# A gated mix of a long convolution and a linear attention on one core: wide PSUM pairs, four-term products, and a new order

## The chip, the core and the metric

The kernel runs on one core of one Trainium2 chip. A core has engines with instruction streams of their own: TensorE (PE; its weight loads are shown as PEld), VectorE (DVE), ScalarE (ACT), GpSimd (POOL) and SyncE (SP), which issues most DMAs. They meet through semaphores. The metric is the device time of one execution in microseconds (us). "Before" is the kernel as it stood, "after" the changed one.

## What is computed

The output is `g*a + (1-g)*b` for an input `u` of 2048 rows (time) by 512 columns (channels), all in bf16, where `a` is a state-space long convolution, `b` a linear attention, and `g` a gate with one value per row:

```python
g = _sigmoid((x * gate_w).sum(-1, keepdims=True))            # x is A_u
# a: per channel d, 128 complex states n
K = jnp.einsum("dn,dnl,dn->dl", Cc, jnp.exp(dt * A * l), dt * Bc).real   # 512 x 2048
a = irfft(rfft(pad(u.T, 4096)) * rfft(pad(K, 4096)))[:, :2048].T + u * Dskip
# b: 32 heads of 16, q, k, v = x @ wqkv
pq, pk = q @ w_phi, k @ w_phi                                # per head, 16 x 16
phi = concat(softmax(p), softmax(-p))                        # 32 features, of pq and of pk
num = phi_q @ (phi_k.T @ v);  den = phi_q @ phi_k.sum(rows) + 1e-6
b = (num / den) @ wo
```

## The kernel before

Line numbers are those of the kernel before, as the profile shows them.

**How the work is put in order.** Nothing is issued where it is written. Each piece of work (a group of matmuls, an eviction, a product, a DMA) is a node, made by `Plan.add` (L111) or `Plan.dma` (L132). It names its engine, the nodes it depends on, the buffers that it takes and drops, and for some ACT nodes the activation table set that it needs (`tab`: "T" for sines, "L" for exponentials and logarithms). `Plan.run` (L153) then issues the nodes in the order that the string `ORDER` (L74) gives, two digits in base 64 for each node. That order was made ahead of time by a planner that is not part of the kernel. `SIDES` holds one digit for each movable node: mostly ACT or DVE for a copy out of PSUM (`Plan.copy`, L147: ACT's at L149, DVE's at L151), in some cases DVE or POOL (`Plan.vec`, L144). `RINGS` holds a digit for each node that may take its PSUM tile from one of two rings. `WARM` (all zeros here) could put idle matmuls ahead of some nodes (`heat`).

**PSUM.** The rings are two double banks for the whole kernel ("ps"), two more double banks that change hands: first "p0" (for the preparation), then three single banks "bk" and one bank "acc" (for keys and early queries), and last two double banks "pf".

**Stages.** `prepare` (L199) loads the parameters, builds the Fourier tables and the polar coefficient tables C, D and G (L383 to L438), and transposes the input to xT (L504). Its sines need table set T, its exponentials L. `fold` (L517) multiplies w_phi into the q and k weights (wtp L530, wps L546): WW then holds folded key weights and the value weights, Wqp the folded query weights. `keys_and_spectrum` (L560) takes the input's spectrum in two stages of matmuls (psAu L591, psBu L616) and writes it to DRAM as XUd; the copies of their results are XAu and xst. `attention_keys` (L660) goes through eight pairs of row tiles (128 rows each). For each tile it projects the keys into one bank (pk L709), takes two exponentials of 512 columns for the two signs (Ek L711), sums them (on PE by L730 for pairs with a 1 in `ZPS`, else on DVE), takes the reciprocal by Ln and Exp, projects the values (vp L757), copies them (vb), multiplies them by the reciprocal (vr L766) and adds up kv (kvp L774).

`plan_queries` (L814) takes four query blocks of 512 rows; 0, 1 and 2 are early and take their tiles from "bk", 3 is late and takes double banks. A block projects (pq L843), takes exponentials (Eq L846), computes denominators (zs, L863 to L889) and turns them into the scales apm (aw L899). These go to DRAM as apd (ar) and come back spread over partitions as ax; then DVE multiplies Eq by ax (em L913), and PE makes num (ops L923) and the product with wo (bps L946 to L953). Block 3's gated rows (outL) are stored at L995.

`plan_conv` (L1060) works in 16 units of 32 channels. For a unit the nodes are: sines cs (`plan_tables`, L1008 to L1026), exponentials E (`plan_exp`, L1035 to L1053), two products A1 and A2 (L1101), a sum A3 of their halves (L1112) for some units, two products R (L1119, L1123), the matmuls kps of the convolution kernel (`kgen_chunk`, L175, L183), its copy KD, the first Fourier stage psA (L190) and its copy XA. Twelve units go by fours through `transform` (L1193), 128 columns of the output at a time; the last block is cut into units (12, 13), 14 and 15. `transform` does the second Fourier stage psB (L196), its copy XK, the products t with the spectrum XUX (L1233, L1236), the first inverse stage psz (L1265), its copy Zr, a transposition over DRAM (Zd written, ZT read, L1287), for the last piece of work a near path without DRAM, the second inverse stage psy, and the mix with the gate (ou, L1362 to L1371), whose rows are stored at L1382.

Whether A3 is issued hangs on the string `FOURS`, one digit a unit: with a 0 the two halves of A are added on DVE and PE takes two product terms, with a 1 PE takes four:

```python
terms = [(k, k) for k in range(2)] if not four else [(0, 0), (2, 0), (1, 1), (3, 1)]
an.append(P.add("DVE", "A3", (lambda: None) if four else a3, an[-1:]))
```

**Table sets.** ACT holds one table set at a time. The loads (L65, by `act.begin`) are nodes of their own, `tabT` and `tabL`, at the places where `prepare` and `phase` (L1076) put them: one T for the first sines, then L, then T for the coefficients, and so on; in the convolution the sines of four units are one phase, with a load on both sides of it.

Of the kernel before, what the change touches and what calls it, by code (L numbers as in the profile page):

```python
# [70 lines left out]
class Plan:  # L71

    DIGITS = "0123456789abcdefghijklmnopqrstuvwxyzABCDEFGHIJKLMNOPQRSTUVWXYZ-_"
    ORDER = ("040B0H0K0d0y0C0D0L0s0I070J0M0P0g000S110j0N08010z0T0m0Q0e2R0a0p0q0r0_0W2T100U0O0V14120Y2U2x0A2S050k130Z2y2V2X2Z0R190v0t0u"  # L74
             "0b0c0w2_0l0E0X2W1516172L1a061b2Y022-30311y33340n030f0-"
             "0h1e1f0i1w2J18321c0F0o2B2K2M1n1z1H1g1A1o2D2C1d1p1I091x1E1J351Q1R2F1B0x1C2E0G2H1q36372G2I2P382N2Q391F3b2O3c4C1S3a4J4L4K4M"
             "3d3e4Q4R3f4U1Y3g4N1r4O1h4V3h1L4Y4-"
             "4P3i4Z4_3j4W4S53542z57504T3k4X1Z515b5d58521s1D593l5c3n5i5e55565j3m5a1G3o5q5f5g5s5r5t3p3r3q1T5m5n5u3s5v5h5o5k5w5x5B1P4D4E"
             "3w2v5l5p4F5y5F5C3y1U5H3x5G5I5J5z5A1V5D5E3t3z5U3D5K5V5M5N3A3R3E2w3F5W5L1O5_3G5O5Q5X5Y5Z3B3C1W605R5S1N3K3M1K3S1M5-"
             "5P3L634G642A615T653N673T6869626a666m6n6o3U6p3V3W3X3Y6b6c6q6d6r6s1t3Z3H3-1X3_3O1i1j41401_4221431-"  # L80
             "1k1l204445466e272923222b282d4748243P491m2a4a2c2e4b4g2f4c2g4d252h2o4e4h4i4n1u4j3u3v2j4p2i2l2k2m2q2p6i262s4q4o1v4k2n4u2r2t"
             "6f4v4w6j4r3I2u4x4y4z6g4l8l3J4A8p8m6t6u6k6v8q3Q4f4s6x6h8k8o6l8n8r8s6y6z6w6A6C4m4t4B8C6G8t6I6K8w8x8y8u6B6H6J4H8D8v6L6M6N7d"
             "8z8A8E4I8B7e7f8I7g8F6F9e8Q8G8H9b6O6P8R7h7j7i6Q6R8J9f7M7N8S6S6T6U6Vaeaf7O8W8X8K7k9g8L8T8U8Z8-"
             "938M8N7l6D8_7m8V7n6W6X6Y8O8P8Y7P94an7o7pao7q6_70717r90917Qa47S9295ag7R6Z7s6-"
             "72aha8a9966Ea7akaca5ai73aa75979998ajap7677a69aalatamab74ad7TaBaC7t797u7v7U78au7y7z7V7w7x9caq9naras7AavaH7W9d9h9o9paw7X9v"
             "aY9waK7Y7ZaDaL9q9raZ7a9x9y9zaIc57B7-aM9kc69D9EaQaEbX9L7Cb_aF7D9M7_9Ac07EaRaG9iaxaz80ay9B818285bYaA7Ga-"
             "7IaJ86879j9Fc19s7Jb-"
             "9l9m9Na_7bc7aNaOaPc3cbb2b37HbZc283aS9C7FaT849G9H9I9t89aUaWaV8baX7cccc8c99O9u9P9Q9R888cb87Kb9b0c4caceb19J8abacfcgbg8dck9K"
             "8ecl8f8gbbbh8hbcbibob4cP9Sbpbqcd9T8ichci7L8jcBcCcjcsdYcYctcucycDczdZd-cQcR9Ucmd_cHcvcw9W9Xcnbj9VbwbkblbxcocIbre0eLcp9Ze1"
             "e2b5b6eMbse3eUeVcxb7bye4cqbtbu9Ybdbe9-"  # L90
             "9_cAcrcSbme5cZdOdScEbfcFcGcTcUe6a0a1bve7dTdRdWeNa2e8cJcKe9bzbAedeecLeRcNcOa3eSeaebeOcMc_ePbBd0ecd1d7cVd8d9cWeCdfcXeWdPdU"
             "d2daefege-e_eQd3dbdQdgeTdVd4dndodXdhdcg1g2dieDeEdjeXbKfAbCbnbDbEbFeYfBeZf0f1bGc-dpbLddg7dqbHd5f2drbMf3f4f5bNfGbIbJbOezdk"
             "eAfDdsfEeBeIf6f7feffdldtbPdebQdBfCfHehdueifFejdmf8fgeJd6ekdvfIfJdyf9fafhfbg4fifKg5g6dwfjdzfkfcdxdCdEfLdAdFfMg3g8dGg9dHfN"
             "fleFelfdfmfpdDdLgagbgcgddIeGemeKfqeHfOfPfQfRgeenepfneofreqeresgfggghgifSfTfUfofsbRgjbSgkdJftetglfVfYfZgmgngobUbVgqfufWdM"
             "dNbWgpf-fvfxfygreufwevewexbTeydKfzfXf_g0gvgwgsgtgugx")
    SIDES = ("011111010010101011001110110010011001010100001011100000000000011000011001111101000100000100000000000000000000000010000000"
             "00100001000000000000000101010000000000000100001101001")
    RINGS = ("001010111111010010100000000000000000000000100000000000000000001101100000000101101011100100100001101010111100111001010100"
             "01111")
    WARM = ("000000000000000000000000000000000000000000000000000000000000000000000000000000000000000000000000000000000000000000000000"  # L100
            "000000000000000000000")
    FOURS = ("0111100101011000")
    ZPS = ("01000111")

    HOT = ("pk", "vp", "pq", "zp", "ops", "bps4", "psA", "psBu", "psB128", "psB64", "psB32", "psz", "pszn", "psyn32", "psy128", "psy64", "psy32", "kps")
# [5 lines left out]
    def add(self, eng, name, fn, deps=(), take=(), drop=(), rw=("", ""), tab=None, sets=None, opens=None, cost=0.0):  # L111
        n = Bag()
        n.eng, n.name, n.fn, n.take, n.drop, n.cost = eng, name, fn, list(take), list(drop), cost
        n.tab, n.sets, n.opens, n.ring = tab, sets, opens, None
# [38 lines left out]
    def run(self):  # L153
# [3 lines left out]
        sides, rings, warm = iter(self.SIDES), iter(self.RINGS), iter(self.WARM)  # L157
        for n in self.nodes:
            n.at = n.eng if isinstance(n.eng, str) else n.eng[int(next(sides, 0))]
            for r in n.take:  # L160
                if not isinstance(r, str):
                    n.ring = r[int(next(rings, 0))]
                elif r in self.psums:
                    n.ring = r
            n.warm = int(next(warm, 0)) if n.name in self.HOT and n.ring in ("ps", "bk", "pf") else 0
        done = set()
# [393 lines left out]
def keys_and_spectrum(P, nc, g, psum):  # L560
# [3 lines left out]
    def bank(name):  # L564
        return g.heat(g.psA.tile([128, 512], F32, name=name, tag="bk"), 2)
# [1062 lines left out]
```

## Time and profile before

| | |
|---|---|
| median of 3 runs | 265.99 us (265.86 to 266.54) |
| the profiled execution | 265.5 us |
| its span in the profile | 263.7 us |
| mean granted TensorE clock | 0.916 |
| DMA | 35.93 MB in 67547 packets, 136 GB/s in the mean |

The profiled execution's span is what the profile's times count from and to; the device time is a little longer. In a row of a timeline stand the start, the duration, the engine, the line, the operation, the tiles written and read with their shapes, the count of instructions that the row sums up, and in brackets an idle time ahead of it with the instruction that ended it. A duration runs from an instruction's start to its end; the next of the same engine may start before that end. A row of a group has the busy time, the mean ns of one, and the idle time ahead of the group.

### The profile page before, as it was taken

To read this page: it belongs to the slowest core of one execution; us is meant where nothing else is said; L and a number is where in the kernel's file an instruction comes from. 1 tells how busy PE (TensorE), PEld (TensorE's weight loads), DVE (VectorE), ACT (ScalarE), POOL (GpSimd) and SP (SyncE) were. 2 spreads that over 40 slices of the span, in tenths; PEclk is the share of its full clock that TensorE was granted. 3 is DMA by queue.
4 is the path that set the end of the run, shared out by engine and by line. 5 is a ranking of instruction groups with operands and counts; after the bars stand their busy time and mean duration, and the time that the engine had idled before them with its cause. 6 is when DMAs were issued, how large, how long until landed. Compare 5 with 4: busy or idle time off the path is not lost.

```text
span 263.7 us, 10050 instructions
## 1 busy us (share of the span) xinstructions
PE 198.5 (75%) x4491; PEld 133.8 (51%) x4512; DVE 233.9 (89%) x315; ACT 221.3 (84%) x305; POOL 8.3 (3%) x21
## 2 busy tenths in 40 slices
PE   0755999999845688988565867889996678979770
PEld 0654656646634423446354245665674456764550
DVE  6799989888799989999999999999999999986630
ACT  6989999998899989998999899999998996744200
POOL 4700000000000000000000000000000000000000
PEclk9999999999995659997999579999999999998975
DMA  6899000454500885203343366239753599989576
GB/s 196 144 204 233 6 4 2 121 146 138 151 10 2 239 239 165 83 13 87 88 162 82 122 209 210 73 116 199 150 193 120 189 239 242 179 206 141 133 112 102
DMA packets 67547, 35.93 MB, mean 136 GB/s; under 512 B 46000, under 2 KB 62000, under 8 KB 67504
## 3 DMA queue, kind: packets, MB, share of 16 engines
q1 hardware_dynamic: 65648, 34.76, 55.0%
q10 hardware_dynamic: 1856, 0.52, 1.1%
q8 instruction: 35, 0.57, 1.0%
q14 instruction: 8, 0.07, 0.1%
HBM read 22.17 MB, written 13.11 MB: 134 GB/s over the span
## 4 chain that ended last, share of the span: by engine, by line
PE 32%; DVE 26%; ACT 13%; DMA 12%; issue 7%; SPq 7%; DVEq 0%; ACTq 0%
PE pk L709 5%; DMA ax<-apd 5%; PE vp L757 5%; DVE A L1101 3%; SPq L1494 3%; DMA ZT<-Zd 3%; DMA apd<-apm 3%; ACT cs L68 3%; DVE R L1123 2%; DVE R L1119 2%; PE psz L1265 2%; PE psA L591 2%; PE bps L946 2%; PE psB L616 2%; PE kvp L774 2%
## 5 line engine op out<-in xcount | busy, mean ns | idle before, releaser
L1101 DVE TENSOR_TENSOR A<-Ctab,Dtab 128x2048 bf16<-128x2048 bf16 x32 | 37.9, 1220 | 0.0
L68 ACT ACTIVATE cs<-args 128x1024 bf16<-128x1024 f32 x32 | 30.8, 1042 | 1.5 <-PE args L1023 1.5
L1265 PE MATMUL psz<-t,TI 128*128 128x512 bf16 x51 | 16.5, 414 | 6.2 <-DVE t L1233 4.6
L1123 DVE TENSOR_TENSOR R<-E,cs 128x2048 bf16<-128x2048 bf16 x16 | 19.5, 1219 | 0.1
L1119 DVE TENSOR_TENSOR R<-E,cs 128x2048 bf16<-128x2048 bf16 x16 | 19.5, 1219 | 0.0
L68 ACT ACTIVATE Ek<-pk 128x512 bf16<-128x512 f32 x32 | 16.7, 600 | 1.9 <-PE pk L709 1.6
L183 PE MATMUL kps<-R,A 128*32 128x64 bf16 x1536 | 17.2, 203 | 1.5 <-DVE A L1112 0.4
L183 PEld LDWEIGHTS <-A 128*32 128x32 bf16 x1536 | 15.3, 117 | 5.6 <-issue 2.0
L149 ACT CAST Zr<-psz 128x1024 bf16<-128x1024 f32 x15 | 15.5, 1032 | 3.2 <-PE psz L1265 1.5
L149 ACT CAST XA<-psA 128x1024 bf16<-128x1024 f32 (+1 forms) x15 | 14.7, 1017 | 3.4 <-PE psA L190 3.4
L757 PE MATMUL vp<-WW,xT 128*128 128x512 bf16 x59 | 16.9, 419 | 0.5 <-issue 0.3
L616 PE MATMUL psB<-XAu,TB 64*128 64x128 bf16 x256 | 11.8, 250 | 6.6 <-ACT xst L149 3.5
L1233 DVE TENSOR_TENSOR t<-XUX,XK 128x2048 bf16<-128x2048 bf16 x14 | 16.7, 1219 | 0.0
L68 ACT ACTIVATE E<-args 128x1024 bf16<-128x1024 f32 x16 | 16.4, 1036 | 0.3 <-PE args L1045 0.2
L68 ACT ACTIVATE Eq<-pq 128x512 bf16<-128x512 f32 (+1 forms) x28 | 16.5, 694 | 0.1
L149 ACT CAST XK<-psB 128x1024 bf16<-128x1024 f32 (+1 forms) x14 | 13.7, 993 | 2.8 <-PE psB L196 1.5
L843 PE MATMUL pq<-xT,Wqp 128*128 128x512 bf16 x64 | 15.4, 379 | 0.8 <-ACT xT L149 0.6
L709 PE MATMUL pk<-WW,xT 128*128 128x512 bf16 x58 | 15.0, 380 | 0.4 <-issue 0.2
L190 PE MATMUL psA<-W,KD 128*64 128x128 bf16 x256 | 10.7, 233 | 5.5 <-ACT KD L149 2.7
L616 PEld LDWEIGHTS <-TB 64*128 64x128 bf16 x256 | 9.7, 111 | 9.9 <-issue 9.8
L196 PE MATMUL psB<-XA,TB 128*128 128x128 bf16 (+2 forms) x192 | 10.6, 206 | 3.6 <-DVE XA L151 1.6
L190 PEld LDWEIGHTS <-KD 128*64 128x64 bf16 x256 | 8.5, 117 | 9.1 <-issue 5.2
(210 smaller groups left out, 502.0 us busy)
## 6 DMA issues: line engine op xcount, KB each, us to landing
XUX<-XUd SPq DMA_DIRECT2D x32, 256.0 KB
XUd<-xst SPq DMA_DIRECT2D x8, 512.0 KB
ax<-apd SPq DMA_DIRECT2D x16, 256.0 KB
Zd<-Zr SPq DMA_DIRECT2D x15, 256.0 KB
ZT<-Zd SPq DMA_DIRECT2D x6, 512.0 KB
UD<-in_A_u_dram SPq DMA_DIRECT2D x16, 128.0 KB
XUd<-xst SPq DMA_DIRECT2D x8, 256.0 KB
wqk<-in_B_wqkv_dram SPq DMA_DIRECT2D x1, 1024.0 KB
```

What stands on the lines that cost most here:

```text
L68: return self.nc.scalar.activation(**kw)
L149: self.nc.scalar.copy(out=o, in_=i)
L183: nc.tensor.matmul(kps[32 * dj:32 * dj + 32, g4, e, :], lhsT=A[:, d // 4, 32 * ka:32 * ka + 32, d % 4], rhs=R[:, kr, d, :], start=(i == 0) ...
L190: nc.tensor.matmul(ps[64 * ri:64 * ri + 64], lhsT=lhsT, rhs=fc.W1[:, ri].rearrange("p r d -> p (r d)"), start=True, stop=True, tile_positi ...
L616: nc.tensor.matmul(box.ps[:, c2, sl, :], lhsT=fc.TB[rows, b0:b0 + 2].rearrange("p a b -> p (a b)"), rhs=X.t[rows, k, r0 + sl].rearrange("p ...
L709: nc.tensor.matmul(box.ps[:], lhsT=xT[:, st, kt, :], rhs=g.WW[:, kt, :], start=(kt == 0), stop=(kt == 3))
L757: nc.tensor.matmul(box.ps[:], lhsT=xT[:, st, kt, :], rhs=g.WW[:, 4 + kt, :], start=(kt == 0), stop=(kt == 3))
L1101: nc.vector.tensor_tensor(out=c.A[:, :, 64 * k:64 * k + 64, :].rearrange("p q (x b) l -> p x b q l", b=8), in0=cf.unsqueeze(2).to_broadcas ...
L1119: nc.vector.tensor_tensor(out=c.R[:, :, :, 32:64], in0=t.E[:, 1].unsqueeze(1).to_broadcast([128, 2, 32, 32]), in1=t.cs[:], op=ALU.mult)
L1123: nc.vector.tensor_tensor(out=c.R[:, :, :, 0:32], in0=t.E[:, 0].unsqueeze(1).to_broadcast([128, 2, 32, 32]), in1=t.cs[:, ::-1, :, ::-1], o ...
L1233: nc.vector.tensor_tensor(out=box.t, in0=Ls[r0 // ns].X[:], in1=box.XK[:].unsqueeze(1).to_broadcast([128, 2, 1024]), op=ALU.mult)
L1265: nc.tensor.matmul(box.ps[:, hb, :], lhsT=fc.TI[:, k].rearrange("p t h a -> p (t h a)"), rhs=box.t[:, k, 512 * hb:512 * hb + 512], start=( ...
```

## The change

The code changes in these points:

- `ORDER`, `SIDES` and `RINGS` are new strings; `WARM`, `HOT` and `heat` are gone.
- `FOURS` is all ones: units 0, 5, 6, 8, 10, 13, 14 and 15 are now four-term too. `ZPS` has its ones at other pairs, four as before.
- Keys and values are handled by pairs of tiles: pk and vp fill a tile of two banks, and Ek, the copies vb, the products vr and the matmuls kn work on a pair at once. Early queries' pq and ops take two banks as well.
- The rings: "ps" stays; of the other four banks, for keys and early queries, one double bank "b2", one "bk" and one "acc". pk, vp, early pq and ops, psAu, psBu, the gate's gps and zps take their tile from "ps" or "b2"; zk and the early bps take "bk". Zk has one buffer for two. Ek, Zk and vr are each taken where they are first written, not with the first pk.
- Table loads are no nodes any more. `Plan.run` loads a set ahead of an ACT node whose `tab` is not the set held. The sines of the convolution are planned by pairs of units instead of phases of four.

```diff
-    FOURS = ("0111100101011000")
-    ZPS = ("01000111")
+    FOURS = ("1111111111111111")
+    ZPS = ("00010111")
...
+            if n.at == "ACT" and n.tab and n.tab != held:
+                held = n.tab
+                self.load_set(held)
             n.fn()
...
-    t1 = P.add("ACT", "tabT", lambda: act.begin(TRIG), rw=("", "act"), sets="T")
+    P.load_set = lambda k: act.begin(TRIG if k == "T" else LN_EXP)
...
+    key2 = ("ps", "b2")
...
-            a = P.add("PE", "psAu", pa, [a] if g4 else uc, take=["ps"] + (["XAu"] if g4 == 0 else []), drop=(["UDp"] if g4 == 7 else []), rw=("W1", ""))
+            a = P.add("PE", "psAu", pa, [a] if g4 else uc, take=[key2] + (["XAu"] if g4 == 0 else []), drop=(["UDp"] if g4 == 7 else []), rw=("W1", ""))
...
-            def pk(st=2 * s2 + u, box=box):
-                box.ps = bank("pk")
+        def pk(s2=s2, box=box):
+            box.ps = psum([128, 2, 512], "pk")
+            for u in range(2):
                 for kt in range(4):
...
+        def ex(K=K, box=box):
+            K.E = g.kwk.tile([128, 2, 2, 512], BF16, name="Ek")
+            for sg in range(2):
+                act(out=K.E[:, :, sg, :], in_=box.ps[:], func=ACT.Exp, scale=(1.0 if sg == 0 else -1.0))
...
+            nc.vector.tensor_tensor(out=K.v[:, :, :, 0:16, :], in0=box.v[:].unsqueeze(2).to_broadcast([128, 2, 2, 16, 32]),
+                                    in1=K.v[:, :, :, 16:17, :].to_broadcast([128, 2, 2, 16, 32]), op=ALU.mult)
...
-        nm = 2 if late else 1
-        for m0 in range(0, 4, nm):
+        ring = psq if late else key2
+        for m0 in range(0, 4, 2):
...
-    def phase(units):
-        out, ra = plan_tables(P, nc, g, psum, units, psq, [sh] if prev else [polar])
-        b = P.add("ACT", "tabT", lambda: act.begin(TRIG), [ra[0][0]] + prev, sets="T", tab="L") if prev else polar
...
+    def sines(units):
+        out, ra = plan_tables(P, nc, g, psum, units, psq, [polar])
         for a, sc, t in ra:
-            t.nc = P.add("ACT", "cs", sc, [a, b], drop=["psum"], tab="T")
+            t.nc = P.add("ACT", "cs", sc, [a], drop=["psum"], tab="T")
...
     for h in range(6):
-        for u in (2 * h, 2 * h + 1):
-            if u in g.PHASES and u:
-                phase(range(u, g.PHASES[u]))
+        sines((2 * h, 2 * h + 1))
...
+            own = {"b2": ("b2", 1), "bk": ("bk", 1), "acc": ("acc", 1)}
+            if P.cur.ring in own:
+                t, n = own[P.cur.ring]
+                return g.psA.tile(shape, dt, name=name, tag=t, bufs=n)
```

In what the order issues, counted over the whole kernel: 16 table loads for 11; 16 key exponentials of 1024 columns for 32 of 512; 16 query exponentials of 1024 for 24 of 512 and 4 of 1024; 8 vr products of 2048 for 16 of 1024; no A3 for 8; 2048 kps matmuls for 1536.

## The prediction

> **What bounds the kernel now.** I read the page's engine shares first, then a table of windows cut where the work changes, then the engines' timelines.
>
> ```profile
> span 263.7 us, 10050 instructions
> PE 198.5 (75%) x4491; PEld 133.8 (51%) x4512; DVE 233.9 (89%) x315; ACT 221.3 (84%) x305; POOL 8.3 (3%) x21
> PE 32%; DVE 26%; ACT 13%; DMA 12%; issue 7%; SPq 7%; DVEq 0%; ACTq 0%
> ```
>
> VectorE (DVE) is busy for 89% and ScalarE (ACT) for 84%, yet the chain that ended last (third line) lies more on TensorE (PE). So no engine bounds the whole; the windows say which does where.
>
> ```profile
> 0.00:29.00 29.00, 14.84 (x164) 12.80 (x166) 24.48 (x57) 25.50 (x32) 8.33 (x21) 1.00 0.91 178
> 29.00:70.00 41.00, 40.47 (x738) 24.80 (x743) 35.88 (x51) 37.87 (x72) 0.00 (x0) 1.00 0.30 86
> 70.00:104.50 34.50, 23.15 (x321) 13.84 (x321) 33.11 (x56) 32.05 (x38) 0.00 (x0) 0.75 0.46 131
> 104.50:241.00 136.50, 108.21 (x2819) 73.91 (x2827) 132.91 (x141) 121.82 (x158) 0.00 (x0) 0.94 0.59 147
> 241.00:263.70 22.70, 11.88 (x459) 8.47 (x456) 7.54 (x12) 4.11 (x7) 0.00 (x0) 0.78 0.69 118
> ```
>
> Columns: window, length, then busy us of PE, PE's weight loads, DVE, ACT, GpSimd; granted clock; DMA share; GB/s. From 29 to 70 PE is full (40.5 of 41.0: projections, keys), and DVE waits 5 us. From 70 to 104.5 PE has 11 us empty and DVE (33.1 of 34.5) and ACT (32.1) do the coefficient tables. From 104.5 to 241 DVE sets the pace, 132.9 of 136.5. After 241 nothing is busy: latencies. The four stretches have three different bounds, so each gets its own sum. The profiled execution took 265.5 us, 1.8 more than its span; the median of the runs is 265.99, 0.5 above that. Sums go against 265.5 and 0.5 is added at the end. About 0.3% (0.8 us) is what a measurement of this kernel can tell from no change.
>
> **Prices.** An instruction costs what it adds behind another of its kind, not its whole duration.
>
> ```profile
> 67.09 2.06 ACT L68 ACTIVATE Ek<-pk 128x512 bf16<-128x512 f32 x4 [0.43 <-PE pk L709]
> 99.39 3.77 ACT L68 ACTIVATE cs<-args 128x1024 bf16<-128x1024 f32 x4 [1.49 <-PE args L1023]
> 99.83 2.37 DVE L1101 TENSOR_TENSOR A<-Ctab,Dtab 128x2048 bf16<-128x2048 bf16 x2
> L1112 DVE TENSOR_TENSOR A<-A 128x2048 bf16<-128x2048 bf16 x8 | 9.8, 1221 | 0.1
> L766 DVE TENSOR_TENSOR vr<-vb,vr 128x1024 bf16<-128x1024 bf16 x16 | 10.5, 686 | 0.5 <-ACT vr L68 0.3
> L151 DVE CAST xst<-psB 128x1024 bf16<-128x1024 f32 x4 | 4.9, 1221 | 0.9 <-PE psB L616 0.9
> L151 DVE CAST vb<-vp 128x512 bf16<-128x512 f32 x9 | 6.1, 687 | 1.9 <-PE vp L757 1.9
> ```
>
> Four 512-wide exponentials take 2.06 (about 0.49 each after the first), four 1024-wide ones 3.77 (0.91). Two A products take 2.37, so one adds 1.14; the 687 ns copies add 0.60.
>
> **The change, part by part.** Counts come from the order in which the two programs issue on each engine.
>
> *Up to the first R product (stage A).* ACT gets five more table loads (16 for 11), +6.4; the key exponentials become 16 of 1024 for 32 of 512, 14.6 for 15.7; the value copies 3 of 1024 for 7 of 512, -0.7; and copies of xT, UDp and xst go to DVE, others come back, -4.6 net. Together ACT's work before its first E is unchanged. DVE gives up 16 vr products for 8 wide ones (9.6 to 9.1), one A3, one E product and selE (to GpSimd), and takes the copies: -0.3. So nothing is won here by work; only empty time can go.
>
> ```profile
> 103.18 1.28 ACT L65 ACT_TABLE_LOAD   x1
> 104.47 1.02 ACT L68 ACTIVATE E<-args 128x1024 bf16<-128x1024 f32 x1
> 106.29 1.22 DVE L1119 TENSOR_TENSOR R<-E,cs 128x2048 bf16<-128x2048 bf16 x1
> 7.38 1.89 PE L530 MATMUL wtp<-ident,wqk 128*128 128x128 bf16 x16 [7.38 <-DMA wqk<-in_B_wqkv_dram]
> 28.02 1.89 PE L709 MATMUL pk<-WW,xT 128*128 128x512 bf16 x7
> ```
>
> By the windows ACT was busy 95.4 of the 104.5 us ahead of E: 9.1 us empty, of which 3.5 before 29. The new order mixes the table work into the PE-bound stretch: one Abs and two Sin of the coefficients stand ahead of the first key exponential, the C products between the key sums. That spreads DVE's and ACT's load over the 29 to 70 stretch, where DVE had 5 and ACT 3 us free. What can't go: ACT starts behind the first DMA, as now; the second half of psB still waits for all XAu copies (3.12 us of PE idle now) and then runs at half clock:
>
> ```profile
> 80.01 1.89 PE L616 MATMUL psB<-XAu,TB 64*128 64x128 bf16 x32 [3.12 <-ACT XAu L149]
> 90.53 0.62 PE L616 MATMUL psB<-XAu,TB 64*128 64x128 bf16 x16 [0.33 <-ACT xst L149]
> ```
>
> (16 matmuls take about 0.95 there against 0.62 later). I leave 5.6 us empty: -3.5, with ends 0 and -6.5. wqk moves from second to eighth on SP's queue and the UD loads behind it, some 3 us later; wtp waits for it, but the folded weights are needed only when pk starts at 28.02, 18.7 us after the first wtp group ends (9.27), so I cost it at nothing, or 3 if that cover is gone.
>
> The loads themselves: does one cost more than its row?
>
> ```profile
> 71.73 0.31 ACT L68 ACTIVATE vr<-Zk 128x128 bf16<-128x128 f32 x1
> 72.04 1.28 ACT L65 ACT_TABLE_LOAD   x1
> 73.33 2.01 ACT L68 ACTIVATE trg<-pb 128x1024 bf16<-128x1024 f32 x2
> ```
>
> The load starts as the one before ends (71.73 + 0.31) and the next starts 0.01 after it: 1.28 each. The Trainium skill, "ScalarE: Activation LUTs", section "What ACT_TABLE_LOAD costs", adds a drain of about 1.38 us to every switch, 2.66 in all, and its "Table sets: the hidden batching unit" advises against alternating sets; by it the five added loads would be 13.3 us instead of 6.4. The rows around the load show no such drain; the load's 1283 ns agrees.
>
> *From the first R to the first t pair of the last unit (stage B), 106.29 to 240.66.*
>
> ```profile
> 239.38 1.28 DVE L1236 TENSOR_TENSOR t<-XUX,XK 128x1024 bf16<-128x1024 bf16 x2
> 217.16 0.73 PE L183 MATMUL kps<-R,A 128*32 128x64 bf16 x64
> 209.69 1.26 PE L183 MATMUL kps<-R,A 128*32 128x64 bf16 x128
> ```
>
> The string of four-term units holds 16 ones, so no A3 is issued any more: seven A3 fewer in this stage, 7 x 1.14 = 8.0. DVE also loses three 512 copies of ops (1.8) and wins back copies of KD, XA, bps and Y; net -6.2. In exchange eight units (0, 5, 6, 8, 10, 13, 14, 15) get 128 matmuls for 64: 8 x 0.53 = 4.2 us on PE, which has 28 us empty here and is given its A 1.14 earlier each time. If that cover is gone it is +4.2. ACT's work falls by about 1 (query exponentials in 1024s), beside DVE.
>
> What is late next: the attention round trip over DRAM.
>
> ```profile
> 116.02 0.43 DVE L886 TENSOR_TENSOR zs<-zs,den 128x256 f32<-128x256 f32 x1
> 116.48 0.38 ACT L68 ACTIVATE apm<-zs 128x256 bf16<-128x256 f32 x1 [0.34 <-DVE zs L886]
> 128.69 2.57 DVE L913 TENSOR_TENSOR Eq<-Eq,ax 128x2048 bf16<-128x2048 bf16 x2
> 194.34 0.38 ACT L68 ACTIVATE apm<-zs 128x256 bf16<-128x256 f32 x1
> 204.86 1.22 DVE L913 TENSOR_TENSOR Eq<-Eq,ax 128x2048 bf16<-128x2048 bf16 x1 [0.30 <-DMA ax<-apd]
> ```
>
> From the end of apm to the Eq product that reads ax it takes 204.86 - 194.72 = 10.1 us. Now 12.2 us of DVE work lie between block 0's last zs step (116.45) and the Eq products at 128.69. In the new order only 8.6 do (R, R, KD, A, XA, A, E, R: five at 1.14, two at 1.13, one at 0.60), so DVE stands for 2 to 4 us with R and A queued behind; kps and the later psA wait for those. I take 3, and 1 for waits on the fuller PE: -6.2 + 4 = -2.2; ends -6.2 and +2.
>
> *The tail.* DVE's work there is 0.5 more (one Zr copy), beside latencies.
>
> ```profile
> 256.59 0.69 DVE L1368 TENSOR_TENSOR xT<-psy,gT 128x512 bf16<-128x512 f32 x1 [0.51 <-PE psy L1343]
> 251.63 6.97 SPq L1382 DMA_DIRECT2D out_dram<-xT  x4
> 258.64 1.10 SPq L995 DMA_DIRECT2D out_dram<-xT  x2
> 259.84 1.26 SPq L1382 DMA_DIRECT2D out_dram<-xT  x2
> 253.16 0.59 ACT L149 CAST Z<-psz 128x512 bf16<-128x512 f32 x1 [4.69 <-DVE Z L151]
> 253.16 5.56 ACTq L1382 DMA_DIRECT2D out_dram<-xT  x4
> ```
>
> The last product ends at 257.28, but SP issues until 261.10 and the span ends 2.6 later, because two outL stores stand ahead of the last two. In the new order outL's stand earlier (two of them on ACT); two stores on SP and two on ACT remain: 257.28 + 1.26 + 2.6 = 261.1, -2.6. ACT has four other stores ahead of its last two; at 5.56 / 4 = 1.39 each from 253.75, the end of that Z copy, all six end at 262.1, and the span at 264.7: +1.0. I take -2.0, since two of ACT's four in that row waited for the last product.
>
> **Sum:** -3.5 - 2.2 - 2.0 = -7.7: 257.8 for the profiled execution, 258.3 for the median; I say 258.0.
>
> **Rivals.**
> - *Slower: the two-bank buffers.* pk and vp fill two banks at a time from three buffers that psA and psB of the spectrum use too, where they had three single banks of their own. A buffer comes back after two 1024 exponentials (1.82) instead of two 512 ones (0.98), or a copy of 1.14 instead of 0.60. If PE, full from 29 to 70, pays the whole difference: 8 x 0.84 + 8 x 0.54 = 11.0; 258.0 + 11.0 = 269.0. For it: PE is the bound there. Against it: two of three buffers stay free while one is emptied, and PE is faster (eight pk or vp matmuls take about 1.8) than ACT. It decides from 0.5 us per fill on.
> - *Stage A keeps its empty time*, because sines and products alternate with the loads: 261.5. For it: ACT was already 93% busy from 29 to 104.5.
> - *No change:* as that, and three added loads stand ahead of sines that DVE waits for: 261.5 + 3 x 1.28 = 265.4.
> - *Deeper:* all lower ends, -6.5 - 6.2 - 2.6 = -15.3, 250.7: the ax trip finds other work and only 2.6 us of ACT's 9.1 stay empty.
> - *Loads that empty the engine:* each added load also costs the work it can't overlap; if that is as much again as the load, 5 x 1.28 = 6.4 more, 264.4. The rows at 72.04 speak against it. It is the rule of the Trainium skill, "ScalarE: Activation LUTs", section "What ACT_TABLE_LOAD costs", weighed above.
> - *The change doesn't do what it says:* a three-term unit left would be worth 1.14; the order shows none.
>
> **How the numbers follow.** Forecast (254 to 260) 0.46; empty time kept 0.16; deeper 0.13; loads that empty 0.02; no change 0.07; buffers 0.16. Faster by over 0.3%: 0.46 + 0.16 + 0.13 + 0.02 = 0.77; within 0.07; slower 0.16. The range goes from the deeper case to just over no change, 250.5 to 266.5; outside lie the slower case and little below.
>
> **What would show it.** In the changed profile: DVE about 228 us busy, no product A<-A, 2048 kps matmuls, 15 loads on the helper's line at 1.28; the first E at 101, the first R at 102.5; an idle of 2 to 4 us ahead of the first Eq product, put to ax; the last t32 pair near 235; two stores on each queue after the last product. Wrong would be: PE waits in front of pk or vp between 29 and 70 that name Ek or vb and sum to over 8 us (buffers); a first E at 104 or later (stage A); gaps around the loads (emptying); waits for kps in front of KD in stage B (PE's cover gone).

## The result and the profile after

The changed kernel takes 281.44 us in the median of four runs (280.24 to 288.41), the kernel before 266.26 beside it: a ratio of 1.054 with a 95% interval of 1.045 to 1.063. The forecast was 258.0, with a range of 250.5 to 266.5. The profiled execution took 282.58 us, its span 280.8. Ratios below are to the kernel before on the same chip, over the executions within 1.5% of their kernel's fastest; in two experiments (a_open, a_sel_rz) the profiled execution is not among these.

The page of the changed kernel, its first lines, the chain that ended last, and the two queues that carry instructions:

```profile
span 280.8 us, 11053 instructions
...
PE 209.1 (74%) x5024; PEld 142.1 (51%) x5024; DVE 229.9 (82%) x302; ACT 218.0 (78%) x264; POOL 10.2 (4%) x22
...
q8 instruction: 39, 0.64, 0.9%
q14 instruction: 8, 0.07, 0.1%
...
PE 35%; DVE 23%; ACT 17%; DMA 12%; issue 10%; SPq 2%; DVEq 0%; ACTq 0%
```

DVE did 4.0 us less work (229.9 for 233.9; the forecast was about 228), yet the time grew by 15. TensorE (PE) did 10.6 us more, and "issue", time in which an engine waits for nothing that the profile shows, went from 7% to 10% of the chain. The windows, cut at the first R and at the first t of the last piece:

```profile
0.00:29.00 29.00, 12.77 (x125) 11.43 (x126) 23.37 (x56) 21.52 (x27) 10.15 (x22) 0.88 0.85 178
29.00:70.00 41.00, 39.87 (x661) 24.20 (x659) 39.33 (x51) 39.99 (x57) 0.00 (x0) 0.96 0.19 52
70.00:108.60 38.60, 26.98 (x464) 16.31 (x463) 33.67 (x52) 34.53 (x39) 0.00 (x0) 0.87 0.51 151
108.60:255.57 146.97, 114.72 (x3360) 81.68 (x3360) 124.37 (x132) 120.01 (x139) 0.00 (x0) 0.91 0.56 141
255.57:280.80 25.23, 14.81 (x420) 8.43 (x419) 9.15 (x14) 1.91 (x4) 0.00 (x0) 0.70 0.50 84
```

The same two marks in the kernel before:

```profile
106.29:239.38 133.09, 104.92 (x2798) 72.51 (x2801) 129.94 (x135) 120.03 (x156) 0.00 (x0) 0.94 0.59 149
239.38:263.70 24.32, 13.50 (x466) 9.22 (x464) 8.83 (x15) 4.11 (x7) 0.00 (x0) 0.78 0.74 121
```

Stage A is 2.3 us longer (108.60 for 106.29), stage B 13.9 (146.97 for 133.09), the tail 0.9. In stage B DVE, which set the pace, does 5.6 us less and stands empty for 22.6 us where it was empty for 3.2. So the question is what holds it. TensorE's timeline after, the rows whose idle time is put to issue:

```profile
184.79 0.26 PE L176 MATMUL kps<-R,A 128*32 128x64 bf16 x8 [3.09 <-issue]
...
209.67 0.35 PE L176 MATMUL kps<-R,A 128*32 128x64 bf16 x18 [2.78 <-issue]
...
228.31 0.59 PE L176 MATMUL kps<-R,A 128*32 128x64 bf16 x48 [1.61 <-issue]
...
244.98 0.57 PE L1316 MATMUL psy<-ZT,TJ 64*32 64x128 bf16 x28 [1.98 <-issue]
...
249.81 0.62 PE L176 MATMUL kps<-R,A 128*32 128x64 bf16 x52 [2.05 <-issue]
...
268.85 0.28 PE L1272 MATMUL psz<-TI,t 128*32 128x64 bf16 x3 [1.52 <-issue]
...
273.40 0.21 PE L1329 MATMUL psy<-Z,TJ 64*32 64x16 bf16 x7 [1.47 <-issue]
```

These stops come in the middle of a group of equal matmuls (the kps of 184.79 had 120 of its 128 done), where nothing is left to wait for. With the smaller ones they add up to 16.4 us; in the kernel before to 2.6, and its one large row is this:

```profile
235.62 0.51 PE L1343 MATMUL psy<-ZT,TJ 64*32 64x128 bf16 x22 [1.43 <-issue]
```

DVE's longest waits in stage B follow them (3.01 us at 185.11, 3.22 at 210.07, 3.73 at 250.55, each for kps). The view of waits of the changed kernel:

```profile
PE kps L176 <- issue: 10.4, 7, 3.1
...
DVE A L1074 <- PE kps L176: 6.2, 2, 3.2
...
DVE Eq L895 <- DMA ax<-apd: 5.2, 3, 2.9
```

(engine, what waited, for whom: us in total, times, longest.) What the stop is, the view of DMA shows for 181.6 to 184.9 us:

```profile
q1 hardware_dynamic: 1464, 0.75, 117.2%
q8 instruction: 1, 0.02, 2.9%
```

Beside the data goes one packet of instructions, 16 KB. The queue brought 39 such packets, and TensorE has 10,070 recorded instructions (matmuls, weight loads and a few waits): 258 for a packet. In the trace's packet records that packet runs from 181.72 to 183.23; TensorE stopped at 181.70 and started again at 184.79, 1.56 after it had landed. The same holds for the others: packet 207.28 to 208.26, next matmul 209.67; 225.37 to 226.89, next 228.31; 247.49 to 248.43, next 249.81; 271.04 to 271.97, next 273.40. The stops come 256 recorded instructions apart or a multiple of it. So the theory from here on, "code": TensorE runs out of instructions. A four-term kps is 128 matmuls and 128 weight loads, a whole block of code, gone in 1.3 us. Its rival, "order": the new order has waits of its own (ax, psB, the store of XUd), and the stops cost nothing. TensorE's granted clock, 0.89 in the mean for 0.92 before, is a third candidate; the runs below bear on it too.

The Trainium skill, "Runtime: NRT & Kernel Launch", section "Instruction fetch mechanics", describes blocks of 16 KiB or 256 instructions that are fetched while the one before runs, and calls the cost mostly hidden. The blocks agree with the 39 packets here; the hiding does not hold for blocks that run through in 1.3 us.

### The profile page after: what moved, and what is told of

Read it like the earlier page. It is cut to its first block, busy times and chain, and to the rows that moved or that the text cites. A ratio compares the mean times of both kernels' runs of the same rounds, so it can differ in the third digit from the quotient of the medians.

```text
span 280.8 us, 11053 instructions
## 1 busy us (share of the span) xinstructions
PE 209.1 (74%) x5024; PEld 142.1 (51%) x5024; DVE 229.9 (82%) x302; ACT 218.0 (78%) x264; POOL 10.2 (4%) x22
## 4 chain that ended last, share of the span: by engine, by line
PE 35%; DVE 23%; ACT 17%; DMA 12%; issue 10%; SPq 2%; DVEq 0%; ACTq 0%
DMA XUX<-XUd 6%; DVE A L1074 5%; PE pk L697 4%; ACT cs L68 4%; PE vp L741 4%; PE kps L176 3%; PE psz L1238 3%; PE psA L183 2%; DVE R L1096 2%; DVE t L1206 2%; ACT L65 2%; DMA ax<-apd 2%; DVE R L1092 2%; PE psB L189 2%; DMA XUd<-xst 1%
## 5 line engine op out<-in xcount | busy, mean ns | idle before, releaser
L176 PE MATMUL kps<-R,A 128*32 128x64 bf16 x2048 | 23.9, 202 | 14.0 <-issue 10.4
L176 PEld LDWEIGHTS <-A 128*32 128x32 bf16 x2048 | 21.0, 116 | 18.8 <-issue 14.5
L1238 PE MATMUL psz<-t,TI 128*128 128x512 bf16 x60 | 15.8, 393 | 2.6 <-ACT cs L68 1.5
L140 ACT CAST XK<-psB 128x1024 bf16<-128x1024 f32 x14 | 13.9, 1017 | 3.3 <-PE psB L189 3.3
L68 ACT ACTIVATE Ek<-pk 128x1024 bf16<-128x1024 f32 x16 | 15.4, 1025 | 1.2 <-PE pk L697 1.2
L68 ACT ACTIVATE Eq<-pq 128x1024 bf16<-128x1024 f32 x16 | 15.4, 1045 | 0.0
L183 PE MATMUL psA<-W,KD 128*64 128x128 bf16 x256 | 11.8, 245 | 4.5 <-DVE KD L142 1.3
L140 ACT CAST Zr<-psz 128x1024 bf16<-128x1024 f32 x14 | 14.1, 1023 | 1.2 <-PE psz L1238 0.7
L741 PE MATMUL vp<-WW,xT 128*128 128x512 bf16 x64 | 14.8, 380 | 0.0
L605 PE MATMUL psB<-XAu,TB 64*128 64x128 bf16 x256 | 9.8, 229 | 5.8 <-ACT xst L140 4.5
L895 DVE TENSOR_TENSOR Eq<-Eq,ax 128x2048 bf16<-128x2048 bf16 x8 | 9.8, 1223 | 5.4 <-DMA ax<-apd 5.2
```

The lines of the kernel that those rows point to most:

```text
L68: return self.nc.scalar.activation(**kw)
L140: self.nc.scalar.copy(out=o, in_=i)
L176: nc.tensor.matmul(kps[32 * dj:32 * dj + 32, g4, e, :], lhsT=A[:, d // 4, 32 * ka:32 * ka + 32, d % 4], rhs=R[:, kr, d, :], start=(i == 0) ...
L183: nc.tensor.matmul(ps[64 * ri:64 * ri + 64], lhsT=lhsT, rhs=fc.W1[:, ri].rearrange("p r d -> p (r d)"), start=True, stop=True, tile_positi ...
L741: nc.tensor.matmul(box.ps[:, u, :], lhsT=xT[:, 2 * s2 + u, kt, :], rhs=g.WW[:, 4 + kt, :], start=(kt == 0), stop=(kt == 3))
L1238: nc.tensor.matmul(box.ps[:, hb, :], lhsT=fc.TI[:, k].rearrange("p t h a -> p (t h a)"), rhs=box.t[:, k, 512 * hb:512 * hb + 512], start=( ...
```

## The experiments

**1 to 4. TensorE's code with all else held.** Two runs change only the number of kps matmuls, each in one of the two kernels; two change it as the kernels themselves can, with A3 given or taken.

a_two, in the changed kernel:

```diff
-                kgen_chunk(nc, K.ps[:, cc], c.A, c.R, four)
+                kgen_chunk(nc, K.ps[:, cc], c.A, c.R, False)
```

> The changed kernel with two product terms in the kps matmuls of all 16 units and still no A3 (two of the four terms are left out, so this is its time without half of its kps instructions; everything else, the order too, is the changed kernel's). Theory 'code': TensorE's instructions come by DMA in packets of 16 KB, about 258 instructions each by the trace (39 packets for 10,070 instructions), and a four-term kps is one such packet in 1.3 us; the idle times of 1.5 to 3.1 us put to 'issue' (16.4 us in TensorE's timeline, 2.6 before) are waits for the next packet. Without 2048 of the 10,070 instructions they fall below 5 us and the time from 281.4 to 266-270. Rival 'order': the new order's own waits (ax 5.2 us, psB, XUd) are the loss; kps lies beside other work: 278-281.

268.62 us, ratio 1.008 (1.003 to 1.013): 12.8 us less than the changed kernel, with issue stops of 6.8 us for 16.4 (less than 5 was expected). Of the packets on the instruction queue 31 are left of 39: 8 fewer for 2048 instructions, so 256 in each. The time is what "code" gave, at a granted clock of 0.909 in the profiled execution, lower than the 0.916 before. But TensorE also has 15.7 us less work here (busy 193.4 for 209.1), so this run alone does not part its stops from its work. The windows of this run, between the same marks:

```profile
108.36:241.39 133.03, 101.34 (x2327) 69.36 (x2336) 124.59 (x131) 119.05 (x139) 0.00 (x0) 0.95 0.62 157
241.39:265.30 23.91, 13.25 (x419) 8.08 (x419) 9.06 (x14) 1.91 (x4) 0.00 (x0) 0.71 0.49 82
```

Stage B is back to 133.0 us, with DVE's work the same as in the changed kernel; stage A is as long as there.

b_four_keep, in the kernel before:

```diff
-                kgen_chunk(nc, K.ps[:, cc], c.A, c.R, four)
+                kgen_chunk(nc, K.ps[:, cc], c.A, c.R, True)
```

> The kernel before with four terms in kps of all units, while A3 is still issued where it was (the sum is counted twice in eight units; DVE's work and the order are those of before, only TensorE's instructions grow by 1024). Theory 'code': TensorE's issue waits grow from 2.6 to 8 us or more and the time to 270-277. Rival 'cover' (the prediction: eight times 0.53 us lie in TensorE's 28 us of empty time): 266.3, at most 266.3 + 4.2 = 270.5, with issue waits as before.

278.10 us, ratio 1.046 (1.036 to 1.055), just above the range that "code" gave: 11.9 us more for 1024 instructions that are 4.2 us of TensorE's work by the forecast's price, in a program that is otherwise the old one. By the page TensorE is busy 7.1 us longer (205.6 for 198.5), so even if all of that lies on the path, 4.8 of the 11.9 are more than its work. The clock is as before (0.912 for 0.916 in the profiled executions), so it is not the cause here. The view of waits has the row that wasn't among the long ones before:

```profile
PE kps L183 <- issue: 7.7, 6, 2.5
```

The issue stops are 15.5 us in all. The prediction's "cover" is refuted by this run alone, since nothing of the new order is in it.

b_fours, in the kernel before:

```diff
-    FOURS = ("0111100101011000")
+    FOURS = ("1111111111111111")
```

> The kernel before with FOURS all ones: no A3, DVE's work 9.1 us less, TensorE 1024 instructions more; order, banks and table loads as before. The prediction's price list gives 266.3 - 8.0 (seven A3 behind the first R) = 258 to 260. Theory 'code': issue waits take most or all of it back: 263-271.

277.46 us, ratio 1.040 (1.027 to 1.053), above what either theory gave. Against the run before it only the eight A3 are gone: DVE is busy 225.6 us for 234.7, and the median falls by 0.6. The intervals of the two ratios overlap almost wholly, and the executions of this run spread from 274.55 to 279.31, so what the 9 us are worth is not fixed more closely than between nothing and some 6 us.

a_foursb, in the changed kernel:

```diff
-    FOURS = ("1111111111111111")
+    FOURS = ("0111100101011000")
```

> The changed kernel with the FOURS string of before: units 0, 5, 6, 8, 10, 13, 14 and 15 have A3 again and two terms. DVE gets 8 x 1.14 = 9.1 us of work back, TensorE loses 1024 instructions. Theory 'code': issue waits of TensorE fall by 7 to 11 us, most of them on the path; 273-280. Rival 'order': nothing is won by that, and DVE pays: 286-290.

281.91 us, ratio 1.060 (1.049 to 1.070): as the changed kernel, between the two expectations. The issue stops fell by 4 us only (12.3), less than expected, while DVE's work grew by 8.6. Stage B of this run, and DVE's longest wait in it:

```profile
108.28:257.21 148.93, 111.09 (x2842) 74.16 (x2850) 132.98 (x139) 119.79 (x139) 0.00 (x0) 0.91 0.56 140
```

```profile
219.37 2.36 DVE L1206 TENSOR_TENSOR t<-XUX,XK 128x2048 bf16<-128x2048 bf16 x2 [4.31 <-DMA XUX<-XUd]
```

This run weighs against the simple form of "code". It has the `FOURS` of before and as many matmuls (4494 recorded for 4491), and yet it is 15.6 us slower than the kernel before: the new order, with its buffers and table loads, loses as much with the old units as with the new ones. In stage B, 15.8 us longer than before, TensorE's issue stops are 8.3 us for 1.9, so the order alone brings them out, at units that were four-term already. The rest is not all stops: DVE stands 4.31 us for a load of XUX, 0.3 in a_two. So "order" holds in part. The number of instructions alone doesn't fix the stops; the next runs show what else does.

**5 and 6. The fetch by itself.** Sixteen four-term kps one behind another, from tables of zeros; all else is left out. In the second, loads run beside them: 49 MB by its page (92 of 512 KB and one of 1 MB), not the 12 that its expectation says, and they go on after the last kps.

```diff
+        for U in range(8):
+            kgen_chunk(nc, ps[0], A, R[0], True)
...
+        for k in range(0):   # range(24) in m_kps_dma
...
+        for U in range(8):
+            kgen_chunk(nc, ps[1], A, R[1], True)
```

> Sixteen four-term kps (2048 matmuls of 128x32 by 64 columns and their weight loads, 4096 instructions) one behind another from tables of zeros, with no other work and no data transfers beside them; all else of the computation is left out. In the changed kernel 128 of them take 1.20 to 1.31 us where they run free. Theory 'code': after the first packets TensorE can't go faster than its instructions come: by the lone fetches of the changed kernel's trace 0.9 us from the entry into a block to the next packet, 0.95 for the packet and 1.4 to the first instruction, so about 3.3 us for each 256 instructions, some 50 us in all, with idle times put to issue of about 2 us between. Rival (the issue idle times have another cause, such as semaphores of the dense kernel): about 16 x 1.3 = 21 us, no gaps.

TensorE's timeline of m_kps, where each row is one block of code:

```profile
10.13 1.91 PE L176 MATMUL ps<-R,A 128*32 128x64 bf16 x128 [1.77 <-issue]
13.59 1.91 PE L176 MATMUL ps<-R,A 128*32 128x64 bf16 x128 [1.55 <-issue]
17.32 1.90 PE L176 MATMUL ps<-R,A 128*32 128x64 bf16 x128 [1.82 <-issue]
...
62.06 0.64 PE L176 MATMUL ps<-R,A 128*32 128x64 bf16 x33 [1.82 <-issue]
```

Each block of 256 instructions is followed by a stop of 1.55 to 2.10 us, with no data moving (DMA share 2%) and nothing to wait for. From 10.13 to 62.06 are 14 blocks: 3.71 us each, for the 3.3 expected. (128 matmuls take 1.90 us here and 1.3 in the kernels; why was not looked into, so the rate is told from block to block.)

> The same sixteen kps, the last eight beside 12 MB of loads on SP's queue that start when the first eight are done. Theory 'code, and the packets queue behind data': the last eight take longer than the first, 4 to 5 us for each 256 instructions, since in the changed kernel the packet came 2.0 to 2.7 us after the entry where DMA was busy, for 0.9 to 1.2 elsewhere. Rival 'code alone': both halves alike, about 3.3 us each.

The loads did not wait for the first half as meant: they ran from the start, and one that had to wait left a pause in the middle. That serves as well. Two stretches of windows (length, busy us of PE, its weight loads, DVE, GpSimd, clock, DMA share, GB/s), and the rows at their seam:

```profile
13.43:40.29 26.86, 9.52 (x640) 8.76 (x640) 0.26 (x1) 0.00 (x0) 0.50 0.97 308
40.29:47.48 7.19, 3.81 (x258) 3.51 (x257) 0.69 (x1) 0.00 (x0) 0.50 0.23 65
```

```profile
35.47 1.91 PE L176 MATMUL ps<-R,A 128*32 128x64 bf16 x128 [4.57 <-issue]
40.29 1.90 PE L176 MATMUL ps<-R,A 128*32 128x64 bf16 x128 [2.92 <-issue]
43.75 1.90 PE L176 MATMUL ps<-R,A 128*32 128x64 bf16 x128 [1.55 <-issue]
47.48 1.91 PE L176 MATMUL ps<-R,A 128*32 128x64 bf16 x128 [1.83 <-issue]
54.22 1.90 PE L176 MATMUL ps<-R,A 128*32 128x64 bf16 x128 [4.84 <-issue]
```

While the loads run the stops are 2.9 to 5.1 us; in the pause, with the DMA engines at 23%, 1.55 and 1.83 (and 1.82 in a second one, at 84.81). From 13.43 to 40.29, at 97%, are five blocks of 5.37 us each, more than the 4 to 5 expected; over all 14 blocks, from 13.43 to 84.81 with the pauses, it is 5.10 (DMA 89%). So code waits behind data, as the first theory there said, though by another comparison than planned. The granted clock is 0.50 here and 1.00 in m_kps, and 128 matmuls take 1.90 us in both: neither their time nor the stop in the pause follows the clock.

**7. The same program, the blocks shifted.**

```diff
+                if U == 0:
+                    kgen_chunk(nc, K.ps[:, cc], c.A, c.R, False)
                 kgen_chunk(nc, K.ps[:, cc], c.A, c.R, four)
```

> The changed kernel with 128 more TensorE instructions ahead of the first kps (unit 0's two-term products made once more, then written over; about 0.7 us of TensorE at 113 us). Nothing else moves, but every later 256-instruction block ends half a block earlier in the program. Theory 'code': the idle times go with the block ends. Where the trace of the changed kernel puts block ends 128 instructions earlier, blocks run through in under 4.5 us end at 115.5, 148.7, 174.9, 190.4, 200.5, 239.8, 250.5, 266.0 and 274.5 us: there the new idle times, those at 184.8, 209.7 and 228.3 gone; the time may go up or down by several us (280 to 292). Rival 'transfers of data at these places hold TensorE up': the same instructions stall as before, 282.

TensorE's timeline of it, the first of its stops:

```profile
118.28 0.26 PE L176 MATMUL kps<-R,A 128*32 128x64 bf16 x7 [1.96 <-issue]
...
152.60 0.22 PE L176 MATMUL kps<-R,A 128*32 128x64 bf16 x1 [2.12 <-issue]
178.75 0.39 PE L176 MATMUL kps<-R,A 128*32 128x64 bf16 x22 [1.52 <-issue]
191.34 0.73 PE L189 MATMUL psB<-XA,TB 128*128 128x128 bf16 x10 [3.78 <-issue]
195.08 0.35 PE L176 MATMUL kps<-R,A 128*32 128x64 bf16 x10 [1.28 <-issue]
```

TensorE's rows start 3 to 7 us later at these places, behind the stops, but the count of its instructions settles which is which: the stops at 118.28, 152.60, 178.75 and 195.08 come at the instructions that the changed kernel ran at 115.5, 148.7, 174.9 and 190.4, as foreseen; later ones at 246.5, 256.4 and 277.3 answer to 239.8, 250.5 and 274.5. Two that were foreseen did not come (200.5, 266.0), two came that were not (191.34, 273.3), and the kps that stopped at 184.8, 209.7 and 228.3 run through. 285.53 us, ratio 1.071 (1.064 to 1.078). The stops go with the ends of the blocks, not with the data beside them; and 128 instructions that are 0.7 us of work moved the time by some 4 us. That a_foursb has fewer instructions but other block ends may be why it gained so little; no run shows it.

**8. Table loads.**

```diff
                 self.load_set(held)
+                if n.name == "cs" and "cs" not in self.k.get("seen", ()):
+                    self.k["seen"] = ("cs",)
+                    for _ in range(4):
+                        self.load_set("L")
+                        self.load_set("T")
```

> The changed kernel with eight more table loads ahead of the first sine of the convolution, where ScalarE sets the pace (nothing else changed). At the row's 1.28 us each the first cs, the first E and the first R come 10.3 us later: first R at 118.9 for 108.6. By the Trainium skill, page 'ScalarE: Activation LUTs', section 'What ACT_TABLE_LOAD costs' (a drain of about 1.38 on top), it would be up to 21.3: first R at 129.9.

ScalarE's timeline:

```profile
95.69 11.59 ACT L65 ACT_TABLE_LOAD   x9
107.29 1.02 ACT L68 ACTIVATE cs<-args 128x1024 bf16<-128x1024 f32 x1
```

Nine loads in 11.59 us, 1.288 each, and the sine starts 0.01 after them. First R at 117.1; the stretch ahead of the loads was 1.8 shorter in this run, so the shift is the 10.3 expected. 290.75 us in its one run. The rule of the Trainium skill, "ScalarE: Activation LUTs", section "What ACT_TABLE_LOAD costs", that a switch drains the pipe for 1.38 us besides, is not borne out here.

**9. All units with two terms.**

```diff
-    FOURS = ("0111100101011000")
+    FOURS = ("0000000000000000")
```

> The kernel before with FOURS all zeros: A3 in all 16 units, two terms everywhere; DVE gets 8 x 1.14 = 9.1 us more, TensorE 1024 instructions less. By the run with four terms beside A3 a four-term unit costs TensorE 11.9 / 8 = 1.5 us on the path in that kernel, for 1.14 that A3 costs DVE. Theory 'code': 266.2 + 9.1 - 8 x 1.5 = 263.4, with room from 261 to 268. Rival 'these eight units have cover, only the other eight had not': 266.2 + 9.1 = 275.

273.47 us, ratio 1.022 (1.016 to 1.028), between the two and above the 261 to 268 that "code" left room for. A3 costs DVE 9.2 us more (243.1 busy for 233.9), of which 5.9 show by the ratio; so the eight four-term units of the kernel before would cost TensorE (9.2 - 5.9) / 8 = 0.4 us each on the path, where the other eight cost 11.9 / 8 = 1.5. The granted clock is lower here than before (0.88 for 0.91), which can be part of the 5.9. That it matters which unit, by what stands around its kps and where the blocks end, is the likely reading and not shown. No version of `FOURS` that was run beats the string of before.

**10 to 14. Stage A and ax.** Four edits of the changed kernel's order and sides, and one of them with half the kps.

```diff
 a_sel, a_open, a_sel_rz, a_sel_rz_two:
-    SIDES = ("1111111101111000...
+    SIDES = ("0111111101111000...
 a_open (wqk's nodes 0A 0B 0C, wT's 2P):
-    0g0h0K0i ... 1u1x0A0B0C2O ... 1d1n13141G1y1H0O1V1e2P
+    0g0h0A0B0C0K0i ... 1u1x2O ... 1d1n132P141G1y1H0O1V1e
 a_em (two Eq products, 6y and 71):
-    7T6y8U5X8W8V977J7U7M        8s718z8AaJaL6h8m728g8h8i9u8n8t9r73
+    7T8U5X8W8V977J7U6y7M        8s8z8AaJaL6h8m728g8h8i9u8n8t9r7173
 a_sel_rz, a_sel_rz_two (Ln and Exp, 5A):
-    4j5z2j4k4m4r4l4n2k4t5A4u
+    4j5z5A2j4k4m4r4l4n2k4t4u
```

The reason for the first: DVE in the opening of the changed kernel,

```profile
13.69 1.69 DVE L262 TENSOR_SCALAR tgsv<-tgs,if,one 128x32 int32<-128x32 f32 x1
15.29 2.35 DVE L408 TENSOR_SCALAR pb<-pt 128x256 int32<-128x256 f32 x4
17.57 1.52 DVE L338 TENSOR_TENSOR ppy<-ppy 128x512 bf16<-128x512 f32 x1
```

and GpSimd beside it:

```profile
13.44 1.90 POOL L449 TENSOR_TENSOR selE<-m,b 128x1024 bf16<-128x1024 bf16 x1
...
17.37 1.17 POOL L472 TENSOR_TENSOR diagD<-ident,Dcol 128x512 bf16<-128x512 bf16 x1
```

> The changed kernel with selE back on DVE. In its trace three DVE instructions that run beside GpSimd's selE and diagD (13.4 to 18.5 us) take 1.69, 2.35 and 1.52 us, where the same take 0.30, 0.89 and 0.68 before, and ScalarE and TensorE wait behind them (1.6 and 4.8 us). Theory 'GpSimd slows DVE in the opening, and ScalarE's chain carries it to the first E': first R from 108.6 to 106 or 107, the time 1 to 3 us less, though DVE gets 1.14 us of selE. Rival 'later slack absorbs it': first R and time unchanged within 1 us.

279.06 us, ratio 1.044 (1.040 to 1.048); first R at 106.6. The profile moves as the theory says, by 2.0 us; the time by 2.4, but the intervals of the two ratios overlap. The small tgsv takes 0.43 again and the four pb 1.88; ppy still takes 1.52, so its delay is not selE's. The Trainium skill, "SBUF — State Buffer", section "SBUF: two separate sides", says of the port pair that DVE, in some kinds of instruction, shares with GpSimd that whichever starts first holds it for its whole instruction while the other blocks; the tgsv that ends at 15.38, just after selE at 15.34, agrees.

> As the run with selE on DVE, and wqk third on SP's queue instead of eighth and the first wT copy ahead of the C coefficients' first product, so that the folded weights are there some 6 us earlier (first pk at 28 instead of 30.9). Theory 'the opening (ScalarE 21.5 us busy of the first 29, before 25.5) is what stage A lost': first R at 103.5 to 105.5, the time 3 to 5 us less. Rival 'ScalarE is full behind it in any case, or the parameters come later for it': first R not below 106.5.

Ratio 1.053 (1.044 to 1.063): nothing won; first R at 110.1. With the 1 MB of wqk ahead, ld comes later, and the new order puts an exponential of ld first on ScalarE, which then stands for 5.13 us at the start instead of 2.75, at a granted clock of 1.00 until 10 us. The rival, "the parameters come later", holds.

> The changed kernel with two of the Eq products that wait for ax (1.73 us at 129.3 and 2.85 at 163.6) each moved behind the next two or three DVE instructions that don't need it. Theory 'these waits are part of the loss in the stage that DVE sets': 2 to 4 us less. Rival 'TensorE, held by its code, sets the pace there': within 1 us of the changed kernel's 281.4, the waits turned into waits for kps and psA.

284.58 us, ratio 1.058 (1.051 to 1.064), nothing won either. The waits for ax fell from 5.2 to 0.8 us, and DVE waited 3.70 for kps, 3.61 for bps and 2.75 for the denominators instead: here a wait that was taken away turned into others.

> As the run with selE on DVE (first R at 106.6, 279.1 us), and the last but one Ln and Exp of the key sums, with the table load ahead of them, issued on ScalarE before the xst copy that waits 2.8 us for an XUd store at 91.7 instead of behind it. Theory 'ScalarE's idle times carry through to the first E': the load and the two activations (1.9 us) fall into the wait; first R at 104.5 to 105, the time 1 to 2 us less than with selE alone. Rival 'the store or TensorE holds up the sines in any case': first R unchanged, 279.

First R at 106.1, where 104.5 to 105 was expected. One execution took 273.59 us, the other three 279.53 to 283.89, so there is no verdict on the time.

> The same with two product terms in all kps and no A3 (two of four terms are left out). Theory 'the losses are separate: 12.8 us by code, 2.4 by selE, 1 to 2 by that wait': 268.6 - 2.4 - 1.5 = 264.7, below the kernel before. Rival 'they overlap, DVE or ScalarE sets the pace once code does not': 267 to 269.

268.62 us, ratio 1.010 (1.003 to 1.017): as a_two. First R came at 105.8 instead of 108.4, and stage B took 138.0 us instead of 133.0. The rival holds: what stage A gives is not passed on, even with half the kps.

| run | TensorE's matmuls recorded | A3 | issue stops of TensorE, us | median, us | ratio |
|---|---|---|---|---|---|
| before | 4491 | 8 | 2.6 | 266.26 | 1 |
| changed | 5024 | 0 | 16.4 | 281.44 | 1.054 |
| a_two | 3982 | 0 | 6.8 | 268.62 | 1.008 |
| a_foursb | 4494 | 8 | 12.3 | 281.91 | 1.060 |
| b_four_keep | 5003 | 8 | 15.5 | 278.10 | 1.046 |
| b_fours | 5003 | 0 | 13.9 | 277.46 | 1.040 |
| b_fours0 | 3979 | 16 | 2.4 | 273.47 | 1.022 |

## Why the prediction was wrong

- **The step that failed** is a term put at nothing: what TensorE pays for the instructions of the kps bursts. The prediction priced the eight more four-term units at "8 x 0.53 = 4.2 us on PE, which has 28 us empty here", and "if that cover is gone it is +4.2". The 0.53 is what 64 more matmuls cost when their instructions are there. Half a block of code more for each unit cost 11.9 us for these eight units in the old order (b_four_keep), and the new `FOURS` alone, priced at some -8, came out 11 us slower (b_fours). Idle time of TensorE elsewhere is no cover, because the stop follows directly upon the burst, and KD, psA and the A buffer wait on it. The profile of before held both signs: 35 packets of instructions on its page, and the 1.43 us put to issue at 235.62.
- **The new order** failed in the same way. Without its 8.0 us of A3 the forecast's sum is 266; with the `FOURS` of before the new order took 281.9 (a_foursb), with TensorE's stops at 12.3 us for 2.6. So the two losses, 11 and 15.6 us, do not add up: together they are 15. With half of the kps in all sixteen units the new order is 12.8 us faster again (a_two). How the loss of the order alone divides into stops, TensorE's own work and waits such as that for XUX stays open.
- **DVE's gain** was right as a sum (stage B: 129.94 to 124.37 us busy, forecast -6.2) and wrong as a time: in the old order with all units four-term, 9 us of it were worth 0.6 by the medians, at most some 6 (b_fours against b_four_keep).
- **Stage A**, forecast at -3.5, came at +2.3. ACT's work ahead of E is indeed the same, but its empty time grew instead of shrinking, above all in the opening (busy 21.5 of 29 us, before 25.5): 2.75 us for ld, 1.58 for pb behind GpSimd's selE, 2.83 later for a store of XUd to free xst. selE was costed as work taken from DVE, without what GpSimd costs DVE beside it: with selE back on DVE the first of the three rows is 1.26 us shorter, the second 0.47, the third no shorter (a_sel). The rows of wqk, costed at nothing "or 3 if that cover is gone": first pk at 30.90 for 28.02. How much of this reaches the end is not settled: 2.0 us earlier at the first R went with 2.4 at the end in a_sel, within the noise, and 2.6 earlier with nothing in a_sel_rz_two, against a_two.
- **The ax trip** came as foreseen at the first place (1.73 us, forecast 2 to 4) and at two more, 5.2 in all for 3. In a_em most of it was taken away, and nothing was won.
- **The tail**: from the last product to the end 5.3 us instead of 6.4, so the store step was right in sign; two stops for code (1.52 and 1.47) lie ahead of that product, and the tail as a whole is 0.9 longer.
- **The rivals**: the buffers, the one slower case, did not come about: pk and vp waited 0.2 us in all, in the groups of the page. The loads cost 1.28, as taken. A rival "TensorE's code" was missing, and with it the right end of the range.
- **What stays open**: with half of its kps, and 6.8 us of stops left, the changed kernel is at 268.6, still above the kernel before, and the forecast's sum made it 258. Stage A accounts for 6 us of this in the profile, the tail for 1.6, stage B for 2; but a_sel_rz_two shows that the first is not simply to be had. In it, too, TensorE has 8.7 us of issue stops. What sets the pace of stage B then was not settled.

## What to carry to other kernels

Count TensorE's instructions where they come thick: small matmuls with a weight load each run through a block of 256 instructions in 1.3 us, and here a block took about 3.7 us from one to the next with no data moving and 5.4 beside full DMA, so trading a product on DVE for such matmuls can be paid in code, whatever TensorE's idle share. The order counts as well as the number: with as many matmuls TensorE's stops were 2.6 us in the old order and 12.3 in the new one. In a profile the sign is an idle time put to "issue" in the middle of a group of equal matmuls, 256 instructions after the last or a multiple of it. And a gain on the engine that sets the pace holds only until the next limit, which one run that changes nothing else (b_four_keep) shows before the whole change is made.

## What the runs showed of the hardware that was not expected

- TensorE's instructions come by DMA, in packets of 16 KB with 256 instructions each, and later when data keeps the DMA engines busy: 3.71 us for each 256 instructions with no data beside (m_kps), 5.37 with loads that keep the DMA engines at 97% (m_kps_dma). After a packet landed the next matmul started 1.4 to 1.6 us later in five stops of the changed kernel.
- Where these blocks end matters: 128 instructions more ahead of everything moved the stops to other places and the time by some 4 us (a_pad).
- 128 matmuls of kps took 1.90 us at a granted clock of 1.00 (m_kps) and at 0.50 (m_kps_dma).
- A small DVE instruction took 1.69 us for 0.30 while GpSimd wrote selE (1.90 us), and ended with it.
- Nine table loads in a row took 11.59 us, 1.288 each, and the next activation started 0.01 us behind them (a_loads).
